# Converting half a weight matrix at a time, with two small edits to the planner and the last store

## The chip, the cores and the metric

The kernel runs on one core of a Trainium2 chip. The metric is the device time of one execution in microseconds; the median of three runs is shown. The engines named here are TensorE (PE in the profile, with its weight loads as PEld), VectorE (DVE), ScalarE (ACT), GpSimd (POOL) and SyncE (SP), which issues every data transfer of this kernel.

## The reference

A gated linear recurrence is followed by a multiplicative feed-forward block:

```python
# q, k, v, f_logit: (4, 8, 768, 48)
f = 1.0 / (1.0 + np.exp(-f_logit))
for t in range(S):
    state = f[:, :, t, :, None] * state + np.einsum('bhd,bhe->bhde', k[:, :, t], v[:, :, t])
    y[:, :, t] = np.einsum('bhd,bhde->bhe', q[:, :, t], state)
x = y.transpose(0, 2, 1, 3).reshape(3072, 384)
a = x @ w1              # w1, w2: (384, 1024)
b = x @ w2
h = a * b @ w3          # w3: (1024, 1024)
out = h @ w_out         # w_out: (1024, 384)
```

The weights arrive as 64-bit floats (w1, w2, w3 and w_out are products of a random float32 array with a numpy float64 scalar), q, k, v and f_logit as 32-bit floats.

## The kernel before

**Stages.** The sequence is cut into 24 units of 128 steps (`NU`), six for each of four batches. For a unit, `front` (line 474) issues the loads of f, k, q and v, makes the gate on ScalarE (L515), runs two scans on VectorE (L523 forward, L545 backward) and scales k and q with them (L553, L539); the pair products follow on TensorE (L566, L576), a causal mask on GpSimd (L706), the values (L650, L669), the state update (L683; L756, L759, L815 on VectorE) and a move of the result into `xt`, the transposed input of the feed-forward block. Units 0 to 3 come first and close together; units 0 and 1 have forms of their own (L604, L610, L622, L871).

Four units make a block of 512 tokens; there are six blocks. Block 0 does its up products plainly (`part`, line 916): for each of eight groups of columns and each half of the tokens one product with w1, whose result ScalarE copies (L931), and one with w2, multiplied into the copy on VectorE (L936). Blocks 1 and 2 use seven products in place of eight (`seven`, line 969, products at L990); blocks 3 to 5 use a longer scheme with shared sums (`many`, line 1117, products at L1145, kept results at L1166, sums at L1189). `three` (line 890) is the helper whose matmul is at L894, used by block 0's up products and by all `down` products (line 1225). w3 and w_out are folded into one matrix `wc` on TensorE first (L1477), so that the down step is one product by `wc`; VectorE makes four sums of it (L1523) and ten of w1 and w2 (L1509).

**Weights.** `fetch` (line 1367) loads a piece of 64-bit words into a large tile called `place` and turns it into 32-bit floats by four instructions: ScalarE makes the low bits (L1415, `rest`); VectorE shifts the high words into a region of magnitudes (L1418, `shifted`), joins sign and low bits into the destination (L1422, `signed`), and adds the magnitudes to it (L1428, `joined`). `weights` (line 1447) calls it for w1 and w2, which are read as four halves: A is columns 0 to 511 of w1, B the same of w2, C and D the other columns of w1 and w2. Each half is three pieces of 128 rows and 512 columns (`KM` = 3). `EARLY = "23ACBD"` gives the order in which VectorE takes units 2 and 3 and the four halves. Pieces take their places in `place` from the list `halves`, ten places of 1024 words; a load waits for the `signed` step of whoever had an overlapping place (`holders`, line 1363). `folding` (line 1462) does the same for four pieces of w_out (768 columns) and eight of w3 (1024 columns), at `2048 * ((load_no + 1) % NRAW)`.

**The order.** All work is given to `Plan` as tasks with a cost, dependencies and a priority; `listed` (line 181) repeatedly takes the task that could start first, ties going to the lower priority number, and so fixes each engine's order. The chip's real waits are semaphores between the instructions in that order. Transfers go to SP's queue and take one of eight lanes, weight loads also one of three heavy lanes (`moves`, line 461). `plan.pool("t", ...)` hands out the places for the kept results of `many`; `temporary` (line 384) maps its first four numbers to `firsts` and `ups`, which the sevens use too. Where the plan leaves TensorE idle in the first 130 us, `idle` (L396) emits products of a constant, one for each 0.43 us of the planned gap, each of two instructions.

The end: `down(i)` writes two output tiles of 128 rows, `o1` and `o2`; `store` (line 1308) sends each by one transfer. In the last one m3, the last product, is emitted together with a read of the flag `left` into a register of every engine.

Of the kernel before, what the change touches and what calls it, by code (L numbers as in the profile page):

```python
# [36 lines left out]
F32 = mybir.dt.float32  # L37
# [45 lines left out]
EARLY = "23ACBD"  # L83
CROWDED = [(6.0, 19.5, (1.35, 1.85)), (33.0, 46.0, (1.3, 1.3))]
# [190 lines left out]


def up_weights(w12, which, kc, jc):

    return w12[:, which, kc, jc * P : jc * P + P]
# [12 lines left out]
def ranged(ctx, tc, q, k, f_logit, v, w1, w2, w3, w_out, out, ident, w12, wc, left):  # L292
# [47 lines left out]
    halves = [a + i for a in (0, 2048, 4096, 8192, 10240) for i in (0, 1024)]  # L340
# [30 lines left out]
    plan.slot("ab", 4)  # L371
    moving = plan.add("PE", 0.0, lambda: None, takes=["ab"], prio=-1e9)
# [101 lines left out]
    def front(u):  # L474
# [4 lines left out]
        ask = [ask, ask + 0.5, ask + 1.0, n0 - (28.2, 28.2, 28.2, 28.2, 12)[min(u, 4)] if u in (0, 1) or u > 3 else ask + 1.2]  # L479
# [419 lines left out]
    def ffn(n):  # L899
# [190 lines left out]
        def w_view(i):  # L1090

            if i < KM * 4:
                return w12[:, :, i // 4].rearrange("p w (h g b c) -> p w h g b c", h=2, g=2, b=2)[:, :, i % 4 // 2, :, i % 2]
            return home(W_SUMS[i - 4 * KM][3]).rearrange("p (w g c) -> p w g c", w=2, g=2)
# [130 lines left out]
        def down(i):  # L1225
# [82 lines left out]
            def store(half):  # L1308
                def emit():
                    t0 = n * TB + (i + half * UB // 2) * P  # L1310
                    nc.sync.dma_start(out[t0 : t0 + P], q["o1" if half == 0 else "o2"])
                return emit
# [32 lines left out]
            for half, deps in ((1, ("c21", "c22")), (0, ("c11", "c12"))):  # L1345
                stores.append(moves(1, 197, 300, store(half), [q[nm] for nm in deps], -10))
# [20 lines left out]
    def fetch(loads_, a, prio, subs, deps=()):  # L1367

        total = subs[-1][1]
        if not wide:
            def plain():
                for place_, src in loads_:
                    for c0, c1, dst, _, _ in subs:
                        d = dst().rearrange("p (a m) -> p a m", a=a)
                        m = (c1 - c0) // a
                        b0 = c0 // a if len(subs) > 1 else 0  # L1380
                        nc.sync.dma_start(d[place_], src[:, :, b0 : b0 + m])
            waits = [d for sub in subs for d in sub[4]]
            ld = plan.add("SP", 1.9 * total / 512, plain, waits, prio, lag=2.0)
            return [ld] * len(subs)
        load_no = len(users)
        if load_no < 2 * 2 * KM:
            where = halves[load_no % len(halves)]
        else:
            where = 2048 * ((load_no + 1) % NRAW)
        raw = at(where, 2 * total).bitcast(U32)  # L1390
        words = raw.rearrange("p (n two) -> p n two", two=2)
        held = holders(where, 2 * total)

        def load():
            for place_, src in loads_:
                nc.sync.dma_start(raw.rearrange("p (a m) -> p a m", a=a)[place_], src.bitcast(U32))

        ld = moves(1, total, 400, load, held + list(deps), prio, SURE, lanes=("lane", "heavy"))
        asked.append(ld)
        got = []  # L1400
        users.append((where, 2 * total, got))
        ends = []

        def sub(c0, c1, dst, due, waits):
            n = c1 - c0
            w = n / 512
            lo, hi = words[:, c0:c1, 0], words[:, c0:c1, 1]
            a0 = spot[0] if n <= 512 else (spot[0] + 512) // 1024 * 1024 % 2048
            spot[0] = (a0 + (512 if n <= 512 else 1024)) % 2048
            m = magnitudes[:, a0 : a0 + n]  # L1410
            mine = range(a0 // 512, (a0 + n + 511) // 512)
            s = {}

            def rest():
                nc.scalar.activation(lo.bitcast(F32), lo, AF.Copy, bias=2.0, scale=2.0**-51)  # L1415

            def shifted():
                nc.vector.tensor_scalar(m.bitcast(U32), hi, 3, None, ALU.logical_shift_left)  # L1418

            def signed():  # L1420
                s["to"] = dst()
                nc.vector.scalar_tensor_tensor(  # L1422
                    s["to"].bitcast(U32), hi, 0x80000000, lo, ALU.bitwise_and, ALU.bitwise_or
                )

            def joined():
                to = s["to"].bitcast(I32)
                nc.vector.tensor_tensor(to, m.bitcast(I32), to, ALU.add)  # L1428

            past = [joins[i] for i in mine if i in joins]  # L1430
            e = plan.add("ACT", 0.2 + 0.43 * w, rest, [ld], due)
            h = plan.add("DVE", 0.16 + 0.27 * w, shifted, [ld] + past, due, shared=True)
            g = plan.add("DVE", 0.16 + 0.53 * w, signed, [e, h] + list(waits), due)
            j = plan.add("DVE", 0.16 + 0.53 * w, joined, [h, g], due - 1, shared=True)
            parts.append((g, j))
            joins.update({i: j for i in mine})
            got.append(g)
            ends.append(j)

        for one_ in subs:  # L1440
            sub(*one_)
        return ends

    def w12_part(which, kc, c0):
        return lambda: w12[:, which, kc, c0 : c0 + KH * P]

    def weights():
        due = dict(zip(((0, 0), (1, 0), (0, 1), (1, 1)), DUE))
        pieces.update({key: [] for key in due})
        for item in (x for x in EARLY if x in "ABCD"):  # L1450
            half, which = divmod("ABCD".index(item), 2)
            w = (w1, w2)[which]
            if True:
                for kc in range(KM):
                    c0 = half * KH * P
                    src = w[kc * P : kc * P + P, c0 : c0 + KH * P].unsqueeze(1)
                    pieces[which, half] += fetch(
                        [(slice(0, P), src)], 1, turn_of("ABCD"[2 * half + which]) + 0.02 * kc,
                        [(0, KH * P, w12_part(which, kc, c0), due[which, half] + 0.02 * kc, [])],
                    )  # L1460

    def folding():
        done = []
        for i in range(0, KF, 2):
            src = w_out[i * P : (i + 2) * P].rearrange("(kc p) c -> p kc c", p=P)
            done += fetch([(slice(0, P), src)], 2, 25 + 2.2 * i, [(
                0, 2 * DM, lambda i=i: wos[:, i : i + 2].rearrange("p a c -> p (a c)"), 45 + 2.2 * i,
                holders(10240, KF * DM) + [tk[3][nm] for nm in "qvs"],
            )], [tk[3]["z"]] if BEHIND and i < BEHIND else [])
# [23 lines left out]
        for jc in range(KF):  # L1493
            src = w3[jc].unsqueeze(1)
            got = fetch([(slice(0, P), src)], 1, 36 + 6 * jc, [(
                0, KF * P, w3_piece(jc), 50 + 6 * jc, fp[jc - 2 : jc - 1] if jc >= 2 else holders(8192, 2048),
            )])
# [4 lines left out]
        def sum_up(i, which):  # L1502
            def emit():
                t = w12t[:, which]
                b11, b21, b31, b12, b22, b32 = (
                    w12[:, which, kc, half * KH * P : half * KH * P + KH * P] for half in range(2) for kc in range(KM)
# [143 lines left out]
def convert(ctx, tc, w1, w2, w3, w_out, w12, wc):  # L1650
# [21 lines left out]
    for which, w in enumerate((w1, w2)):  # L1672
        for kc in range(KM):
            single(w[kc * P : kc * P + P], w12[:, which, kc])
# [347 lines left out]
```

## Time and profile before

| | us |
|---|---|
| median of 3 runs | 464.27 (464.22 to 465.06) |
| the profiled execution, its own time | 464.53 |
| its span, first to last instruction | 462.80 |
| PE busy | 454.1 |
| DVE busy | 364.8 |
| ACT busy | 208.2 |
| POOL busy | 64.7 |
| first product of the feed-forward block (L894) | 31.36 |
| end of the last product | 458.1 |

The profile is of one execution. A line of a timeline or of the chain gives the start and the duration in us, the engine, the tile, the line of the kernel and how many instructions are merged; in a group of instructions the last number is the mean in ns of one. "issue" is time in which the engine waited for nothing that the profile shows. Fillers (L396) count as busy.

### The profile page before, as it was taken

What the parts mean: (1) busy time and instruction counts of PE and PEld (TensorE: products, weight loads), DVE (VectorE), ACT (ScalarE), POOL (GpSimd) and SP (SyncE); (2) the same over time, 40 slices, a digit from 0 to 9 for tenths busy, and PEclk for the clock granted to TensorE, in tenths of its full rate; (3) what the DMA queues carried; (4) which work ended last, traced back from release to release, by engine and by line L of the source; (5) the groups of instructions that cost most, each with busy time, mean ns of one, the idle gap of its engine ahead of it and who ended that gap; (6) DMA issues with size and microseconds to landing.
All of it is one profiled execution on the core that took longest, in us unless ns stands there. A gap on an engine that the chain in (4) does not pass through costs nothing.

```text
span 462.8 us, 11767 instructions
## 1 busy us (share of the span) xinstructions
PE 454.1 (98%) x4800; PEld 395.6 (85%) x4800; DVE 364.8 (79%) x657; ACT 208.2 (45%) x468; POOL 64.7 (14%) x90
## 2 busy tenths in 40 slices
PE   8999999999999999999999999999999999999995
PEld 6778885666899888889998889998889988889995
DVE  8998999999898999989983598894669377767641
ACT  4565344532234444442432356664654666675000
POOL 9330001121122332322322000000000000000000
PEclk9999999999999999999999999999999999999999
DMA  6899899743246764445424335634135623330111
GB/s 181 269 297 306 268 343 276 260 103 87 80 110 192 205 186 113 133 135 166 120 57 113 111 112 178 221 113 149 47 124 176 200 91 92 90 95 0 35 68 40
DMA packets 43165, 68.75 MB, mean 149 GB/s; under 512 B 5201, under 2 KB 28242, under 8 KB 42082
## 3 DMA queue, kind: packets, MB, share of 16 engines
q1 hardware_dynamic: 43106, 67.95, 48.0%
q8 instruction: 39, 0.64, 0.6%
q14 instruction: 20, 0.16, 0.1%
HBM read 58.88 MB, written 9.04 MB: 147 GB/s over the span
## 4 chain that ended last, share of the span: by engine, by line
PE 93%; POOL 2%; DVE 2%; issue 1%; ACT 0%; POOLq 0%; DVEq 0%
PE f L894 26%; PE f L990 14%; PE f L1145 10%; PE f L1477 9%; PE pa L1145 7%; PE py L1145 5%; PE py L894 3%; PE py L650 3%; PE pa L894 3%; PE pa L576 2%; PE pa L683 2%; PE f L590 2%; PE py L669 2%; PE pa L990 1%; POOL ab L434 1%; PE f L396 1%
## 5 line engine op out<-in xcount | busy, mean ns | idle before, releaser
L706 POOL TENSOR_SCALAR_AFFINE_SELECT A<-A 64x512 f32<-64x512 f32 (+1 forms) x46 | 43.4, 943 | 104.0 <-ACT A L700 101.9
L1477 PE MATMUL f<-place 128*128 128x384 f32 x128 | 42.7, 488 | 0.0
L894 PE MATMUL f<-xt,w 128*128 128x256 f32 x192 | 42.1, 380 | 0.0
L894 PEld LDWEIGHTS f<-xt,w 128*128 128x128 f32 x192 | 36.3, 190 | 5.0
L894 PE MATMUL f<-place 128*128 128x192 f32 x216 | 39.5, 328 | 0.0
L1477 PEld LDWEIGHTS f<-place 128*128 128x128 f32 x128 | 23.8, 190 | 15.3
L894 PEld LDWEIGHTS f<-place 128*128 128x128 f32 x216 | 35.4, 190 | 0.5 <-issue 0.2
L990 PE MATMUL f<-xt,w 128*128 128x256 f32 x132 | 34.2, 379 | 0.0
L545 DVE TENSOR_TENSOR_SCAN bwd<-gate,back 112x512 f32<-112x512 f32 x24 | 30.8, 1285 | 0.7
L523 DVE TENSOR_TENSOR_SCAN fwd<-gate,floor 112x512 f32<-112x512 f32 x24 | 30.5, 1271 | 1.1 <-ACT gate L515 0.3
L990 PEld LDWEIGHTS f<-xt,w 128*128 128x128 f32 x132 | 24.8, 190 | 3.1
L842 ACT ACTIVATE ys<-py 112x512 f32<-112x512 f32 x22 | 13.1, 596 | 28.2 <-PE py L669 28.2
L1415 ACT ACTIVATE place<-place 128x512 f32<-128x512 uint32 (+2 forms) x24 | 21.1, 890 | 10.1 <-DMA place<-in_w_dram 7.9
L894 PE MATMUL f<-wc,ab 128*128 128x192 f32 x128 | 23.4, 326 | 0.0
L990 PE MATMUL f<-place 128*128 128x256 f32 x84 | 22.4, 385 | 0.0
L806 POOL TENSOR_TENSOR G<-lasts,gate 112x4 f32<-112x4 f32 x20 | 10.7, 535 | 81.3 <-ACT lasts L528 50.3
L894 PEld LDWEIGHTS f<-wc,ab 128*128 128x128 f32 x128 | 21.4, 190 | 0.4
L515 ACT ACTIVATE gate<-f 112x512 f32<-112x512 f32 x22 | 13.9, 632 | 15.4 <-DVE bwd L545 6.6
L650 PEld LDWEIGHTS py<-A,vt 64*64 64x64 f32 (+1 forms) x672 | 13.3, 127 | 7.3 <-issue 5.6
L650 PE MATMUL py<-A,vt 64*64 64x64 f32 (+1 forms) x672 | 18.1, 223 | 0.2
L1552 ACT ACTIVATE A<-A,back 128x512 f32<-128x512 f32 x23 | 17.9, 778 | 0.3
L990 PEld LDWEIGHTS f<-place 128*128 128x128 f32 x84 | 15.3, 190 | 2.2 <-ACT place L1031 0.2
(345 smaller groups left out, 1046.4 us busy)
## 6 DMA issues: line engine op xcount, KB each, us to landing
place<-in_w_dram SPq DMA_DIRECT2D x21, 512.0 KB, 6.4
A<-in_w_dram SPq DMA_DIRECT2D x19, 512.0 KB, 4.0
place<-in_w_dram SPq DMA_DIRECT2D x8, 1024.0 KB, 6.9
out_dram<-o SPq DMA_DIRECT2D x24, 192.0 KB, 2.3
q<-in_q_dram SPq DMA_DIRECT2D x46, 96.0 KB, 3.0
vt<-in_v_dram SPq DMA_DIRECT2D x23, 192.0 KB, 3.2
k<-in_k_dram SPq DMA_DIRECT2D x44, 96.0 KB, 2.5
yt<-ys SPq DMA_DIRECT2D x44, 96.0 KB, 2.9
```

The costliest lines, as they stand in the source:

```text
L515: nc.scalar.activation(gate[u % 2][:, 0:NQ], fu, AF.Sigmoid)
L523: nc.vector.tensor_tensor_scan(s["P"], gate[u % 2][:, 0:NQ], floor, 0.0, ALU.mult, ALU.max)
L545: nc.vector.tensor_tensor_scan(s["R"][:, ::-1], gate[u % 2][:, NQ:0:-1], back[:, ::-1], 0.0, ALU.mult, ALU.max)
L650: done = nc.tensor.matmul(y_block(u, hp, par, half)[p0 : p0 + w], lhsT=s["v"][half * W : half * W + W, h * D : h * D + w], rhs=s["A"][half ...
L706: nc.gpsimd.affine_select(out=a, in_=a, pattern=pattern, compare_op=ALU.is_ge, fill=0.0, base=0, channel_multiplier=-1,)
L842: nc.scalar.activation(ys, py, AF.Copy, accum_out=ysum[:, u : u + 1])
L894: nc.tensor.matmul(out_, lhsT=lhs[i], rhs=rhs[i], start=start and i == 0, stop=i == len(lhs) - 1, skip_group_check=True,)
L990: nc.tensor.matmul(q[nm][:, which * TH : which * TH + TH], lhsT=lhs[i](which), rhs=rhs[i], start=start and which == 0 and i == 0, stop=i = ...
L1145: nc.tensor.matmul(banks[g, c][:, which * TH : which * TH + TH], lhsT=lhs, rhs=x_node(a), start=first and which == 0, stop=True, skip_grou ...
L1415: nc.scalar.activation(lo.bitcast(F32), lo, AF.Copy, bias=2.0, scale=2.0**-51)
L1477: nc.tensor.matmul(w3s["p", jc], lhsT=w3s[jc][:, kc * P : kc * P + P], rhs=wos[:, kc], start=(kc == 0), stop=(kc == KF - 1),)
L1552: return lambda: nc.scalar.activation(a, a, AF.Sign, bias=small, accum_out=counts[:, i : i + 1])
```

## The change

- `fetch` takes a list of loads and converts them together. Each load still has its own transfer and its own ScalarE step; `shifted`, `signed` and `joined` are one instruction each over all the columns. For w1 and w2 this is 1536 columns in place of three times 512; for w_out and w3 there is one load, as before.
- `w12` is laid out by matrix, half, row block and column, so that a half is contiguous; `up_weights`, `w_view`, `sum_up` and `convert` follow.
- The halves have fixed places, `EARLY_AT`: A and D at 0, C at 3072, B at 8192. `halves` goes. The places of w_out and w3 are the same numbers as before, written out.
- v of unit 3 is asked for behind A's loads and not ahead of them (`VLATE`).
- The first four places of the pool `t` are taken by `aside` until the last two sevens of block 2 have ended.
- The output tile that is stored last goes in two transfers: columns 0 to 191 when `c11` is done, and the others when `c12` is.

```diff
+VLATE = (1.2, 2.05)
+EARLY_AT = {"A": 0, "C": 3072, "B": 8192, "D": 0}
...
-    w12 = const.tile([P, 2, KM, DFF], F32, name="w12")
+    w12 = const.tile([P, 2, 2, KM, KH * P], F32, name="w12")
...
-    halves = [a + i for a in (0, 2048, 4096, 8192, 10240) for i in (0, 1024)]
...
+    aside = plan.add("none", 0.0, lambda: None)
+    plan.pools["t"][0:4] = [aside] * 4
...
-        ask = [ask, ask + 0.5, ask + 1.0, n0 - (28.2, 28.2, 28.2, 28.2, 12)[min(u, 4)] if u in (0, 1) or u > 3 else ask + 1.2]
+        ask = [ask, ask + 0.5, ask + 1.0, n0 - (28.2, 28.2, 28.2, 28.2, 12)[min(u, 4)] if u in (0, 1) or u > 3 else ask + VLATE[u - 2] if u in (2, 3) else ask + 1.2]
...
+            if n == MANY - 1:
+                for q in s["seven"][-2:]:
+                    for nm in ("e11", "e22", "e21", "e12"):
+                        q[nm]["frees"].append(aside)
...
+                if final and half == 0:
+                    stores.append(moves(1, 98, 300, store(0, 0, DH), [q["c11"]], -10))
+                    stores.append(moves(1, 98, 300, store(0, DH, DM), [q["c12"]], -10))
+                    continue
                 stores.append(moves(1, 197, 300, store(half), [q[nm] for nm in deps], -10))
...
-    def fetch(loads_, a, prio, subs, deps=()):
+    def fetch(loads_, where, prio, due, dst, waits=(), deps=()):
...
+        landed, low = [], []
+        for i, (at_, n, src) in enumerate(loads_):
+            def load(at_=at_, n=n, src=src):
+                nc.sync.dma_start(raw[:, 2 * at_ : 2 * (at_ + n)].rearrange("p (a m) -> p a m", a=src.shape[1]), src.bitcast(U32))
+
+            def rest(at_=at_, n=n):
+                part_ = lo[:, at_ : at_ + n]
+                nc.scalar.activation(part_.bitcast(F32), part_, AF.Copy, bias=2.0, scale=2.0**-51)
+
+            landed.append(moves(1, n, 400, load, held + list(deps), prio + 0.02 * i, SURE, lanes=("lane", "heavy")))
+            asked.append(landed[-1])
+            low.append(plan.add("ACT", 0.2 + 0.43 * n / 512, rest, [landed[-1]], due + 0.02 * i))
...
+        h = plan.add("DVE", 0.16 + 0.27 * w, shifted, landed + past, due, shared=True)
+        g = plan.add("DVE", 0.16 + 0.53 * w, signed, [*low, h] + list(waits), due)
+        j = plan.add("DVE", 0.16 + 0.53 * w, joined, [h, g], due - 1, shared=True)
...
+            pieces[which, half] = fetch(
+                [(kc * KH * P, KH * P, w[kc * P : kc * P + P, cols].unsqueeze(1)) for kc in range(KM)],
+                EARLY_AT[item], turn_of(item), due[which, half],
+                lambda which=which, half=half: w12[:, which, half].rearrange("p k c -> p (k c)"),
+            )
```

More of the change, by code (lines that the diff above doesn't have):

```diff
@@ L277, in up_weights @@
 def up_weights(w12, which, kc, jc):
-    return w12[:, which, kc, jc * P : jc * P + P]
+    return w12[:, which, jc // KH, kc, jc % KH * P : jc % KH * P + P]
 def place_of(jc):
@@ L1092, in w_view @@
             if i < KM * 4:
-                return w12[:, :, i // 4].rearrange("p w (h g b c) -> p w h g b c", h=2, g=2, b=2)[:, :, i % 4 // 2, :, i % 2]
+                return w12[:, :, i % 4 // 2, i // 4].rearrange("p w (g b c) -> p w g b c", g=2, b=2)[:, :, :, i % 2]
             return home(W_SUMS[i - 4 * KM][3]).rearrange("p (w g c) -> p w g c", w=2, g=2)
@@ L1306, in c12, with store @@
                 nc.vector.tensor_tensor(q["o1"][:, DH:DM], q["Z"], dns["u2"], ALU.add)
-            def store(half):
+            def store(half, c0=0, c1=DM):
                 def emit():
                     t0 = n * TB + (i + half * UB // 2) * P
-                    nc.sync.dma_start(out[t0 : t0 + P], q["o1" if half == 0 else "o2"])
+                    nc.sync.dma_start(out[t0 : t0 + P, c0:c1], q["o1" if half == 0 else "o2"][:, c0:c1])
                 return emit
@@ L1365, in holders @@
         return [g for a, m, gs in users if a < where + n and where < a + m for g in gs]
-    def fetch(loads_, a, prio, subs, deps=()):
-        total = subs[-1][1]
+    def fetch(loads_, where, prio, due, dst, waits=(), deps=()):
+        total = sum(n for _, n, _ in loads_)
         if not wide:
             def plain():
[L1376 to L1389, printed above, removed]
+                d = dst()
+                for at_, n, src in loads_:
+                    nc.sync.dma_start(d[:, at_ : at_ + n].rearrange("p (a m) -> p a m", a=src.shape[1]), src)
+            return [plan.add("SP", 1.9 * total / 512, plain, list(waits), prio, lag=2.0)]
@@ L1390, in fetch @@
         raw = at(where, 2 * total).bitcast(U32)
-        words = raw.rearrange("p (n two) -> p n two", two=2)
+        pairs_ = raw.rearrange("p (n two) -> p n two", two=2)
+        lo, hi = pairs_[:, :, 0], pairs_[:, :, 1]
         held = holders(where, 2 * total)
[L1394 to L1398, printed above, removed]
@@ L1399, in fetch @@
-        asked.append(ld)
         got = []
         users.append((where, 2 * total, got))
[L1402 to L1445, printed above, removed]
+        landed, low = [], []
[8 more added lines that the diff above has]
+            low.append(plan.add("ACT", 0.2 + 0.43 * n / 512, rest, [landed[-1]], due + 0.02 * i))
@@ new lines, in fetch, with shifted, signed @@
+        w = total / 512
+        a0 = spot[0] if total <= 512 else (spot[0] + 512) // 1024 * 1024 % 2048
+        if a0 + total > 2048:
+            a0 = 0
+        spot[0] = (a0 + (total + 511) // 512 * 512) % 2048
+        m = magnitudes[:, a0 : a0 + total]
+        mine = range(a0 // 512, (a0 + total + 511) // 512)
+        s = {}
+        def shifted():
+            nc.vector.tensor_scalar(m.bitcast(U32), hi, 3, None, ALU.logical_shift_left)
+        def signed():
+            s["to"] = dst()
+            nc.vector.scalar_tensor_tensor(
+                s["to"].bitcast(U32), hi, 0x80000000, lo, ALU.bitwise_and, ALU.bitwise_or
+            )
@@ new lines, in joined @@
+        def joined():
+            to = s["to"].bitcast(I32)
+            nc.vector.tensor_tensor(to, m.bitcast(I32), to, ALU.add)
+        past = [joins[i] for i in mine if i in joins]
+        h = plan.add("DVE", 0.16 + 0.27 * w, shifted, landed + past, due, shared=True)
+        g = plan.add("DVE", 0.16 + 0.53 * w, signed, [*low, h] + list(waits), due)
+        j = plan.add("DVE", 0.16 + 0.53 * w, joined, [h, g], due - 1, shared=True)
+        parts.append((g, j))
+        joins.update({i: j for i in mine})
@@ L1447, in weights @@
+        got.append(g)
+        return [j]
     def weights():
         due = dict(zip(((0, 0), (1, 0), (0, 1), (1, 1)), DUE))
-        pieces.update({key: [] for key in due})
         for item in (x for x in EARLY if x in "ABCD"):
@@ L1452, in weights @@
             w = (w1, w2)[which]
[L1453 to L1460, printed above, removed]
+            cols = slice(half * KH * P, (half + 1) * KH * P)
+            pieces[which, half] = fetch(
+                [(kc * KH * P, KH * P, w[kc * P : kc * P + P, cols].unsqueeze(1)) for kc in range(KM)],
+                EARLY_AT[item], turn_of(item), due[which, half],
+                lambda which=which, half=half: w12[:, which, half].rearrange("p k c -> p (k c)"),
+            )
     def folding():
@@ L1465, in folding @@
             src = w_out[i * P : (i + 2) * P].rearrange("(kc p) c -> p kc c", p=P)
[L1466 to L1469, printed above, removed]
+            done += fetch(
+                [(0, 2 * DM, src)], 2048 * ((13 + i // 2) % NRAW), 25 + 2.2 * i, 45 + 2.2 * i,
+                lambda i=i: wos[:, i : i + 2].rearrange("p a c -> p (a c)"),
+                holders(10240, KF * DM) + [tk[3][nm] for nm in "qvs"], [tk[3]["z"]] if BEHIND and i < BEHIND else [],
+            )
         w3s = {}
@@ L1494, in folding @@
             src = w3[jc].unsqueeze(1)
-            got = fetch([(slice(0, P), src)], 1, 36 + 6 * jc, [(
-                0, KF * P, w3_piece(jc), 50 + 6 * jc, fp[jc - 2 : jc - 1] if jc >= 2 else holders(8192, 2048),
-            )])
+            got = fetch(
+                [(0, KF * P, src)], 2048 * ((17 + jc) % NRAW), 36 + 6 * jc, 50 + 6 * jc, w3_piece(jc),
+                fp[jc - 2 : jc - 1] if jc >= 2 else holders(8192, 2048),
+            )
             fp.append(plan.add("PE", 5.15, fold(jc), got + done + fp[-1:], 0, takes=["f"]))
@@ L1505, in emit @@
                 b11, b21, b31, b12, b22, b32 = (
-                    w12[:, which, kc, half * KH * P : half * KH * P + KH * P] for half in range(2) for kc in range(KM)
+                    w12[:, which, half, kc] for half in range(2) for kc in range(KM)
                 )
@@ L1673, in convert @@
         for kc in range(KM):
-            single(w[kc * P : kc * P + P], w12[:, which, kc])
+            for half in range(2):
+                single(w[kc * P : kc * P + P, half * KH * P : (half + 1) * KH * P], w12[:, which, half, kc])
     rows_ = keep.tile([P, KF, DM], F32, name="rows")
```

## The prediction

> **What bounds the kernel.** I read the page's busy shares and slices first. TensorE is busy for 98% of the span, the granted clock never drops, and no slice between the second and the last falls under 9.
>
> ```profile
> PE 454.1 (98%) x4800; PEld 395.6 (85%) x4800; DVE 364.8 (79%) x657; ACT 208.2 (45%) x468; POOL 64.7 (14%) x90
> ...
> PE   8999999999999999999999999999999999999995
> ...
> DVE  8998999999898999989983598894669377767641
> ...
> PEclk9999999999999999999999999999999999999999
> ```
>
> VectorE is nearly as busy in the first third, but a busy TensorE sets the end. So the second view is the chain of waits in order of time: where is TensorE *not* doing products that the result needs? L396 is the filler, products of a constant[...]; a filler occupies TensorE's queue whether or not its reason still holds.
>
> ```profile
> 23.81 1.35 PE f L871 x12
> 25.17 1.30 PE f L396 x6
> 26.46 0.44 PE py L650 x12
> ...
> 28.41 0.86 issue
> 29.27 0.60 PE pa L683 x20
> 29.87 1.49 PE f L396 x6
> 31.36 2.59 PE f L894 x12
> ```
>
> From 31.36 on, the feed-forward products (L894 and the folds L1477) run gapless; there are three more losses, 0.86 us of filler at 124.78, about 0.5 us at 336.95, and the tail after the last product at 458.1:
>
> ```profile
> 118.11 6.67 PE f L894 x30
> 124.78 0.86 PE f L396 x4
> ...
> 336.95 0.46 issue
> 337.41 0.60 ACT ys L1166
> ...
> 456.78 1.31 PE pa L894 x8
> 458.10 0.02 issue
> 458.12 0.36 DVE o L1306
> ```
>
> So an edit gains only if it moves 31.36 forward, or shortens one of these three. The work itself (as many products as before) does not change.
>
> **Merged conversions.** The third view is VectorE's timeline. A, the first half of w1, is three pieces; the last step of the third ends at 29.26 + 0.69 = 29.95.
>
> ```profile
> 22.95 0.68 DVE L539 TENSOR_TENSOR Q<-place,fwd 112x512 f32<-112x512 f32 x1
> 23.56 0.42 DVE L1418 TENSOR_SCALAR place<-place 128x512 uint32<-128x512 uint32 x1
> ...
> 29.26 0.69 DVE L1428 CUSTOM_DVE_ANT_0 w<-place,w 128x1024 uint16<-128x1024 uint16 x1
> ```
>
> Cost of a step by size, from the groups by shape (512, 768, 1024 columns): shift 419, 552, 681 ns; sign 683, 950, 1220; join 719, 953, 1225. Each 256 columns add about 131, 268 and 270. At 1536 columns that makes 0.94 + 1.76 + 1.76 = 4.46 us, against 3 x (0.419 + 0.683 + 0.719) = 5.46 for three pieces. Neighbouring steps overlap (piece starts at 34.92 and 36.58, 1.66 apart, for a sum of 1.82), so the real saving is nearer 5.0 - 4.25 = 0.75 us per half, 3 us of VectorE over the four. ScalarE's three steps per half stay as they are.
>
> The merge adds waits: the shift now needs all three pieces landed, the sign all three ScalarE steps. Behind them on VectorE stand the state updates of unit 2 (L756, L759, L815). VectorE is busy with unit 3's Q until 23.6 in any case, and A's third ScalarE step starts by 24.98 and ends by 25.6. I lay it out: shift 23.56 to 24.43, unit 2's three updates (0.35 + 0.36 + 0.68) to 25.75, sign to 27.45, join to 29.15. A is ready **0.8 us earlier** than 29.95. If the third piece came after 24.4 this would shrink one for one.
>
> For C and B the margin is larger: TensorE has four products of 1.3 us from A, four from C and a visit (1.4) before it needs B, so at 31.36 + 10.4 + 1.4 = 43.1; B ended at 40.97 + 0.69 = 41.66. Their 1.5 us saved is worth nothing on the path.
>
> **What A's 0.8 us buys.** Before, A was ready at 29.95, yet TensorE began at 31.36: it came to the end of unit 3's products at 29.87 and then had 1.49 us of filler. The number of fillers is the planner's gap divided by 0.43. Working its rules through by hand (for order and filler counts alone; the times are the trace's): A's loads go out one transfer earlier, so its second ScalarE step is placed ahead of the copy of unit 2's scores, which puts unit 2's visit (L650) some 0.5 later in the plan: four fillers at 25.17 in place of three; and A's readiness then stands 0.9 us behind unit 3's end in place of 1.48: two fillers in place of three. A filler is two instructions of 0.216. On the chip: 25.17 + 1.74 (filler), 1.38 (visit), 2.03 (unit 3 with its 0.86 stall), about 1.0 (filler) = 31.3; without the stall 30.45.
>
> The stall of 0.86 is "issue": it stands in the middle of a run of small products and waits for nothing that the profile shows. Instruction blocks come by DMA (q8, 39 packets, 0.64 MB, 16 KB each) through rings then full of weight loads. The Trainium skill ("Runtime: NRT & Kernel Launch", Instruction fetch mechanics) says that crossing a block's boundary is mostly hidden, which speaks against fetching as the cause. By that rule there is no fetch to overlap, the stall stays at its 0.86 and the start at 31.3; by the row, if it is a late block, a filler more ahead of it (0.43) hides as much of it and the start comes at 30.9. I take the row's reading: **-0.45 us**, ends 0 and -0.9.
>
> **Loads.** v of unit 3 goes from ahead of A's three loads to behind them: one issue (0.43 on SP) and 192 KB moved past three. It landed about 4.3 us after its issue at 13.81; behind 1.5 MB (landing by about 22.5) it comes some 5 us later, and is read at 28.1 (L683). Five us of cover; one us beyond would cost one. D's loads now all wait for A's sign step (27.5), before their turn at 32.7: nothing. But places of 3072 columns make w_out's first load, at 2048, wait for D's sign step rather than C's. It went out at 41.88; D's third ScalarE step ended at 44.82 + 0.66 = 45.5, and one sign step of 1.76 behind it makes 47.3, 5.4 us later. w_out's fourth load takes the same place after it; the third waited for D before too (issued 49.57) and comes sooner. Behind the waiting load on SP's queue stand unit 4's f, k and q, wanted only after 68. Cover for w_out: folding starts at 67.9 with five products of block 0 in reserve (those at 118.11). They fill TensorE while VectorE makes the sums of the folded weight, which end at 121.15, so a delay of up to 124.78 - 121.15 = 3.6 us at the fold is free. I cost it at 0, ends 0 and +2.
>
> **The filler at 124.78.** The first down product waits for VectorE's last product of block 0 (L936 at 124.90, 0.42). It must follow the last up product whatever is saved. With VectorE up to 3 us ahead the step may stand less queued; one filler of two drops out at best: **-0.2**, ends -0.86 and +0.4.
>
> **Temporaries.** Before, the planner thought four places free while the sevens used them; the first ScalarE copies into them (278.66 and 284.70) waited for TensorE alone, so the mistake cost nothing there. Giving places out in another order can undo or renew the stall at 336.95, a copy that waited for its place: **-0.2**, ends -0.5 and +0.3.
>
> **Last store.** After the final add ends at 458.48 the store is issued (332 ns), and takes 2.7 to landing; the span ends at 462.80. Halved, it has 96 KB for 192; the other half leaves at about 453.3, while SP waits for `left` anyway.[...] Rows of 96 KB (2.5 to 3.3 medians) against out's 2.3 at 192 KB show no gain at all, though those landed among heavy traffic. I take **-0.25**, ends 0 and -0.4.
>
> **Sum.** -0.45 - 0.2 - 0.2 - 0.25 = -1.1 us. The profiled execution took 464.53 (span 462.80 and 1.73 around it), so 463.4; from the median 464.27, 463.15, and I say **463.1**.
>
> **Rivals.** (1) *Start not moved*, 25%: fillers and stall hold TensorE as before (31.3 above); only the store gains: 464.0. For it: both fillers are fixed counts and A was already waiting at 29.95. Against: A's 0.8 us makes the second count smaller. (2) *Everything falls out*, 17%: stall gone (-0.86), filler at 124.78 gone (-0.86), place stall gone (-0.46), store -0.3: -2.5, 461.8. For it: none is tied to work. Against: a list planner fills one gap and opens another. (3) *The fold comes late*, 7%: w_out's first load goes out 5.4 us later, its conversions of some 2.3 us follow, and the first fold waits; beyond the 3.6 us of cover it costs one for one. At 6 us late, +2.4 and -0.5 elsewhere: 466.2. Against: VectorE is 3 us ahead by then.
>
> **From chances to numbers.** Forecast 51% (its own range 462.6 to 463.6). What a measurement of this kernel can tell from no change is 0.2%, 0.93 us: faster is under 463.34. The forecast's share below that is about four fifths (0.42), with rival 2 0.17 and a little of rival 1: 0.64. Same: the rest of both, 0.29. Slower 0.07. The range reaches to rival 2's 461.8 and past rival 1, 464.4.
>
> **What would show it.** VectorE's 1536-column steps of 0.94, 1.76, 1.76; A's join ending at 29.15; L396 x8 near 25.2 and x4 near 30; the first L894 at 30.9; the issue stall shorter than 0.86; the last store landing 2.4 after issue. Wrong would be an L894 start at 31.3 or later, or TensorE idle between 65 and 125.

## The result: 0.4% faster, and where the profile shows it

The changed kernel took 463.24 us (median of 17 runs, 462.6 to 464.57) against 465.05 for the kernel before in the same comparison; the ratio is 0.996, 95% interval 0.9942 to 0.9978. In a second comparison (the first experiment below) it was 463.48 against 464.50, ratio 0.9973 (0.9962 to 0.9985). The forecast of 463.1 stands, its range too. The profiled execution of the changed kernel was one of its longer ones, 464.25 with a span of 462.52, so it shows only 0.3 us of the difference; the repeat (span 461.25) shows 1.55.

The page of the changed kernel, busy shares and slices:

```profile
span 462.5 us, 11749 instructions
...
PE 452.9 (98%) x4800; PEld 395.5 (86%) x4800; DVE 362.1 (78%) x633; ACT 208.6 (45%) x468; POOL 63.9 (14%) x90
...
PE   7999999999999999999999999999999999999995
```

VectorE has 24 instructions and 2.7 us fewer. TensorE sets the end as before. The line numbers have moved: L399 is the filler, L897 the product that was L894, L686 unit 3's state products, L1415, L1419 and L1425 the shift, sign and join.

The chain of waits of the changed kernel, start and duration in us, at the start of the feed-forward products, at the last filler, and at the end:

```profile
25.17 1.73 PE f L399 x8
26.90 0.44 PE py L653 x13
...
28.84 0.04 issue
28.88 0.67 PE pa L686 x26
29.55 1.06 PE f L399 x4
30.61 3.89 PE f L897 x18
...
118.60 5.38 PE f L897 x24
123.98 0.86 PE f L399 x4
...
452.06 5.21 PE f L897 x32
457.28 0.02 issue
457.30 0.36 DVE o L1313
```

The fillers are eight and four instructions, as worked out. The stall of 0.86 is 0.04. The first feed-forward product comes 0.75 us earlier than before, the last one ends 0.82 us earlier (457.28 against 458.10), so nearly nothing was gained between. The filler at 124 is still there. What follows the last product took 5.2 us in this execution against 4.7 before.

VectorE's timeline of the changed kernel, for half A:

```profile
23.89 0.96 DVE L1415 TENSOR_SCALAR place<-place 128x1536 uint32<-128x1536 uint32 x1 [0.25 <-DMA place<-in_w_dram]
24.77 0.35 DVE L759 TENSOR_TENSOR A<-pa,S 112x192 f32<-112x192 f32 x1
...
26.21 1.75 DVE L1419 SCALAR_TENSOR_TENSOR w<-place 128x1536 uint32<-128x1536 uint32 x1
27.99 1.76 DVE L1425 CUSTOM_DVE_ANT_0 w<-place,w 128x3072 uint16<-128x3072 uint16 x1
```

The steps take 0.96, 1.75 and 1.76, against 0.94, 1.76 and 1.76 extrapolated. The shift waited 0.25 for the third piece. A is ready at 29.75, 0.2 earlier than before and not 0.8: the shift started 0.33 later than laid out, the sign step at 26.21 in place of 25.75, and sign and join did not overlap as assumed. A was ready 0.86 us before the first feed-forward product took it (30.61), so on the chip its readiness did not set the start; the fillers did.

In what follows, *first* is the start of the first feed-forward product, *stretch* the time from there to the end of the last product, and *tail* the rest of the span. They are read from the records of each profile; first is up to 0.2 below the chain's number, because the chain starts an instruction where the one before it ends.

| | first | stretch | tail |
|---|---|---|---|
| before | 31.20 | 426.88 | 4.72 |
| changed | 30.44 | 426.82 | 5.26 |
| changed, again | 30.43 | 426.41 | 4.40 |

### The profile page after: what moved, and what is told of

The parts are those of the page before. It is cut to its first block, busy times and chain, and to the rows that moved or that the text cites. A ratio compares the mean times of both kernels' runs of the same rounds, so it can differ in the third digit from the quotient of the medians.

```text
span 462.5 us, 11749 instructions
## 1 busy us (share of the span) xinstructions
PE 452.9 (98%) x4800; PEld 395.5 (86%) x4800; DVE 362.1 (78%) x633; ACT 208.6 (45%) x468; POOL 63.9 (14%) x90
## 4 chain that ended last, share of the span: by engine, by line
PE 94%; POOL 2%; DVE 2%; issue 0%; POOLq 0%; DVEq 0%
PE f L897 25%; PE f L993 15%; PE f L1148 11%; PE f L1464 9%; PE py L1148 6%; PE pa L1148 5%; PE py L897 4%; PE pa L897 4%; PE py L653 3%; PE pa L579 2%; PE pa L686 2%; PE f L593 2%; PE py L672 2%; PE py L993 1%; POOL ab L437 1%; PE f L399 1%
## 5 line engine op out<-in xcount | busy, mean ns | idle before, releaser
L709 POOL TENSOR_SCALAR_AFFINE_SELECT A<-A 64x512 f32<-64x512 f32 (+1 forms) x46 | 42.3, 920 | 110.6 <-ACT A L703 108.5
L897 PE MATMUL f<-xt,w 128*128 128x256 f32 x192 | 42.1, 380 | 0.0
L897 PEld LDWEIGHTS f<-xt,w 128*128 128x128 f32 x192 | 36.3, 190 | 5.0
L1464 PEld LDWEIGHTS f<-place 128*128 128x128 f32 x128 | 23.9, 190 | 15.5
L993 PE MATMUL f<-xt,w 128*128 128x256 f32 x140 | 36.2, 380 | 0.0
L897 PE MATMUL f<-place 128*128 128x192 f32 x192 | 34.8, 327 | 0.0
L897 PEld LDWEIGHTS f<-place 128*128 128x128 f32 x192 | 31.5, 190 | 0.3 <-issue 0.2
L993 PEld LDWEIGHTS f<-xt,w 128*128 128x128 f32 x140 | 26.3, 190 | 3.5
L897 PE MATMUL f<-wc,ab 128*128 128x192 f32 x128 | 23.6, 328 | 0.0
L897 PEld LDWEIGHTS f<-wc,ab 128*128 128x128 f32 x128 | 21.3, 190 | 0.4
L1262 DVE TENSOR_TENSOR place<-ab 128x512 f32<-128x512 f32 x24 | 16.5, 689 | 1.0 <-PE f L897 0.9
```

Source lines behind the costliest of these rows:

```text
L709: nc.gpsimd.affine_select(out=a, in_=a, pattern=pattern, compare_op=ALU.is_ge, fill=0.0, base=0, channel_multiplier=-1,)
L897: nc.tensor.matmul(out_, lhsT=lhs[i], rhs=rhs[i], start=start and i == 0, stop=i == len(lhs) - 1, skip_group_check=True,)
L993: nc.tensor.matmul(q[nm][:, which * TH : which * TH + TH], lhsT=lhs[i](which), rhs=rhs[i], start=start and which == 0 and i == 0, stop=i = ...
L1262: nc.vector.tensor_tensor(abs_[j], x, y, op)
L1464: nc.tensor.matmul(w3s["p", jc], lhsT=w3s[jc][:, kc * P : kc * P + P], rhs=wos[:, kc], start=(kc == 0), stop=(kc == KF - 1),)
```

## The experiments

My theory going in: the time is the first product's start, plus a stretch that is nearly fixed work, plus the tail; the stall ahead of the first product is a late block of TensorE's instructions. The main rival: the 3 us of VectorE that merging saves are the gain, wherever in the span they fall.

**The changed kernel again.** No edit; it gives the other runs something to stand beside.

> The changed kernel once more, on the chip of the runs beside it. Theory (the gain is an earlier first feed-forward product, 0.75 us in the profiles, and a shorter last store): ratio 0.996 to 0.998, first product of L897 at 30.6 again and no stall over 0.3 us ahead of it. Rival (the gain lies in VectorE's relief spread over the span): the first product anywhere, and the stretch from it to the last product shorter than the 426.7 us of both profiles.

Ratio 0.9973 (0.9962 to 0.9985), 463.48 us. First at 30.43, no stall (0.07), as expected. The stretch was 426.41, 0.4 below both earlier profiles: in the first profile of the changed kernel TensorE paused 0.3 us in a run of small products at 208 us, and here it did not.

**The last tile in one store.**

```diff
-                if final and half == 0:
-                    stores.append(moves(1, 98, 300, store(0, 0, DH), [q["c11"]], -10))
-                    stores.append(moves(1, 98, 300, store(0, DH, DM), [q["c12"]], -10))
-                    continue
```

> The changed kernel with its last output tile stored in one transfer again. Theory: the last store takes 2.7 us from issue to landing in place of about 2.4, so 0.25 us slower than the changed kernel (+0.05%). Rival (the fixed part of a transfer is all of it): no difference. Rival (the store is most of the gain that the medians show and the profiles do not): 1 us slower.

463.54 us against 463.48 with two: no difference that the runs can tell. The profile's tail was 4.52 against 4.40. Over all 14 profiles of this study the tails with one store are 4.52, 4.57, 4.72 and 4.77 (median 4.65), with two 4.23 to 4.50 in eight and 5.04 and 5.26 in two (median 4.42). That would be 0.2 us for the split, with a scatter of more than four times as much. In the long tails a few of the store's packets come late: those of the changed kernel began at 458.51 and the last ended at 460.51, against 458.10 and 459.12 in the repeat. Packets of the two instruction queues ran at the same time, but they did so in the repeat too, so what made them late isn't shown. The rival, which puts the whole 1 us on the split, is out.

What the run shows besides is a stall of 0.63 in a program whose first 450 us are the same as in the run before it:

```profile
28.80 0.10 PE pa L686 x3
28.90 0.63 issue
29.53 0.67 PE pa L686 x26
30.19 1.06 PE f L399 x4
31.25 3.89 PE f L897 x18
```

**Three instructions for each merged step, planned anew.** Everything else as changed: layout, places, load order, temporaries, stores.

```diff
-        h = plan.add("DVE", 0.16 + 0.27 * w, shifted, landed + past, due, shared=True)
-        g = plan.add("DVE", 0.16 + 0.53 * w, signed, [*low, h] + list(waits), due)
-        j = plan.add("DVE", 0.16 + 0.53 * w, joined, [h, g], due - 1, shared=True)
...
+        def convert_(i, at_, n):
...
+        for i, (at_, n, src) in enumerate(loads_):
+            convert_(i, at_, n)
```

`convert_` makes the shift, sign and join of one piece three tasks of their own.

> The changed kernel with each piece of 512 columns converted by its own three VectorE instructions; layout, places, loads, temporaries and stores as changed. Theory: A is ready about 0.2 to 0.8 us later than in the changed kernel's profile (29.75), the planner's fillers follow, the first L897 product comes at 30.6 to 31.4, so 0 to 0.8 us slower. Rival (merging is worth its 3 us of VectorE): 1.5 us or more slower.

466.71 us (the profiled execution, 467.8, was its longest), ratio to before 1.0047 (1.0032 to 1.0061): 3.2 us slower than the changed kernel, slower than the kernel before, and a miss for my theory. The rival's number fits. But the profile doesn't show VectorE as the place: first 31.16 (with a stall of 0.63), and a stretch of 429.87, longer by 3.5. In the chain, the folds end at 122.48 in place of about 117, with fewer up products left behind them, then six filler instructions in place of four, and four waits for a place or a bank (a slot of TensorE's output memory) in the last 200 us where the changed kernel has one wait of 0.74:

```profile
122.48 1.29 PE f L897 x6
...
127.25 1.31 PE f L399 x6
...
279.38 0.59 ACT Q L1169
...
380.01 0.46 issue
380.46 0.60 ACT Q L1169
...
404.91 0.46 issue
405.36 0.60 ACT ys L1169
...
413.32 0.46 issue
413.78 0.87 ACT A L1545 x2
...
416.45 0.60 ACT Q L1169
```

At each of the four TensorE pauses 0.46 to 0.84 us for ScalarE's copy, 2.2 in all. So of the 3.5 some 1.5 is in these pauses and 0.4 in the fillers; the rest is spread over delays of 0.1 to 0.2 between products. These places are far from the conversion of w1 and w2. The planner had other tasks and costs and made another order of everything. To know what merging itself is worth, the order has to be held.

**Three instructions for each merged step, in the changed kernel's order.** The tasks and costs stay those of the merged steps; only what they emit is split.

```diff
         def shifted():
-            nc.vector.tensor_scalar(m.bitcast(U32), hi, 3, None, ALU.logical_shift_left)
+            for a, n, _ in loads_:
+                nc.vector.tensor_scalar(m[:, a : a + n].bitcast(U32), hi[:, a : a + n], 3, None, ALU.logical_shift_left)
...
```

`signed` and `joined` are split in the same way.

> The changed kernel in its own order of tasks, with each merged VectorE step emitted as three instructions of 512 columns in a row; everything else as changed. Theory (pieces lost 3.2 us because the planner, given other costs and tasks, made another order, with its waits for places and its fewer reserve products at the end of the folds): A is ready some 0.5 to 0.8 us later, the fillers hide part of that, so 0 to 0.8 us slower than the changed kernel, and the stretch from first to last product stays at 426.4 to 426.9 us. Rival (the three extra VectorE microseconds are what costs): 466 to 467 us again and a stretch near 429.9.

465.86 us (462.87 to 470.16, the widest scatter here; the profiled execution took 464.75), ratio to before 1.0031 (1.0015 to 1.0046). Slower than the changed kernel by 2.4, three times what I had allowed. The stretch was 427.88, neither theory's 426.9 nor the rival's 429.9. The excess in this profile, 1.1 to 1.5 over the changed kernel's two, stands in one place. The waits between 30 and 40 us, and GpSimd's timeline there:

```profile
PEld py L653 <- POOL A L709: 1.3, 1, 1.3
PE py L653 <- POOL A L709: 1.2, 1, 1.2
...
30.56 5.55 POOL L709 TENSOR_SCALAR_AFFINE_SELECT A<-A 64x512 f32<-64x512 f32 x2 [4.73 <-ACT A L703]
```

Unit 3's mask, which GpSimd makes in place, took 5.55 us; it took 1.98 in the profile of the changed kernel and 3.52 in its repeat, where TensorE had work until then. VectorE's three sign, three join and two shift instructions ran back to back from 31.23 to 35.58; the second half of the mask lasted from 31.27 to 36.11. So there was a third theory: what three instructions cost is the mask's turn. The run planned anew does not have this loss, though it has as many VectorE instructions:

```profile
31.02 2.83 POOL L709 TENSOR_SCALAR_AFFINE_SELECT A<-A 64x512 f32<-64x512 f32 x2 [4.75 <-ACT A L703]
```

There VectorE takes the sign and the join of one piece in turn, as in the kernel before (mask 2.17). In both the mask came to an end after a sign step, and the join that needs that sign took 1.02 in place of 0.69. With three signs ahead of three joins no join has to wait for its own sign.

**The same, with C's sign step told to follow the mask.**

```diff
+    pieces[0, 1][0]["deps"][1]["deps"].append(tk[3]["c"])
     ready_at = 0.0
     for t in plan.order():
```

> The run with three instructions per VectorE step in the changed kernel's order, and one dependency more: C's sign step waits for unit 3's mask on GpSimd. Theory (the 2.4 us lost there come from that mask, which took 5.55 us beside back-to-back VectorE steps where it takes 2.0 beside the merged ones, and from TensorE's wait of 1.3 us for it): the mask takes 1.4 to 2.8 us, TensorE does not wait for it at 34.8, the spread of the runs shrinks to about 1.5 us, and the time is 463.3 to 464.3. Rival (three more microseconds of VectorE cost, wherever): 465.5 or more again.

467.64 us (465.68 to 470.13). This did not test it: the planner's dependency orders emission, and since sign step and mask share no data, no semaphore came of it. VectorE's sign step started at 31.30, beside the mask, which took 5.86; TensorE paused 1.7 us for it (starts apart), and then its granted clock fell. It stands as a second sample of the run before.

**The same, with a semaphore.** The first of C's sign instructions waits for the mask, by the helper that the kernel uses for TensorE's row tiles. The planner's dependency of the run before stays in.

```diff
                 done = nc.vector.scalar_tensor_tensor(
...
+                if due == 24.0 and a == 0:
+                    ordered(done, st[3]["masked"])
```

> Three instructions per VectorE step in the changed kernel's order, and now a real wait: the first of C's three sign instructions waits on a semaphore for unit 3's mask on GpSimd. In the run before it, the added dependency only told the planner, and VectorE did not wait. Theory (the 2.4 us lost with three instructions come from the mask, which cannot run beside back-to-back VectorE steps that read two operands): the mask takes 1.4 to 2.2 us in place of 5.6 to 5.9, TensorE has no wait over 0.4 us near 34.5, and the time is 463.3 to 464.5. Rival (three more microseconds of VectorE cost, wherever): 465.5 or more.

463.48 us, ratio to before 0.9983 (0.9972 to 0.9994): 2.4 us faster than the same order without the wait, 4.2 faster than the run before it, from which it differs by the semaphore alone, and level with the merged kernel. The mask took 1.37 us:

```profile
31.71 1.37 POOL L709 TENSOR_SCALAR_AFFINE_SELECT A<-A 64x512 f32<-64x512 f32 x2 [5.81 <-ACT A L703]
...
33.12 1.90 DVE L1421 SCALAR_TENSOR_TENSOR w<-place 128x512 uint32<-128x512 uint32 x3 [0.69 <-POOL A L709]
```

VectorE stood 0.69 us for the mask, has all 24 instructions that merging takes away, and nothing is lost that the runs can tell. So in this order VectorE's microseconds show no worth on the path; the merged steps are worth up to 2.4 us because they leave GpSimd a turn. (This profile had a stall of 1.42 at 28.86; it is the longest of the kernel's runs but one.)

**The sevens' places given out from the start, as before.** The six lines of `aside` are taken out.

> The changed kernel with the four places of the sevens given out from the start, as before. Theory (the places cost nothing where they were taken early, but the order of the last 200 us is solved anew): the stretch from first to last product differs by 0 to 1 us either way, the stall of a copy that waits for its place moves, and the first product stays at 30.6. Rival (the wrong places cost waits at the start of block 3): 0.5 to 1.5 us slower with VectorE or ScalarE waiting between 275 and 300 us.

463.28 us, ratio to before 0.9971 (0.9960 to 0.9982), stretch 426.97. No wait of the kind the rival wanted, and no difference in time. What `aside` is for shows in the last run below.

**The kernel before, one filler more.**

```diff
-                idle(n)
+                idle(n + 1 if 25.5 < t["at"] < 26.5 else n)
```

> The kernel before with four fillers in place of three ahead of unit 2's visit; nothing else. Theory (the 0.86 us stall inside unit 3's state products is a late block of TensorE's instructions, so a filler ahead of it runs in time that was lost anyway): the visit starts at 26.9 in place of 26.46, the stall shrinks to 0.2 to 0.5, and the first feed-forward product still comes at 31.2 to 31.4. Rival (the stall has another cause and stays): first product at 31.8, 0.43 us slower.

464.74 us, ratio 1.0005 (0.9992 to 1.0018). The stall was 0.07 and the first product came at 30.93, 0.27 earlier than before with one filler more. The rival's 31.8 is out. Part of this is luck: TensorE went on at 28.94, against 29.27 before, and a filler can cover a wait but not end it sooner.

**The changed kernel without fillers.** Once without those after 29 us, once without any after 20 us.

```diff
-            if ready_at and n:
+            if ready_at and n and t["at"] < 29.0:
```

> The changed kernel without the fillers ahead of the first feed-forward product and ahead of the first down product (two matmuls each). Theory: the products start when their data is ready, 29.85 in place of 30.61 and 124.6 in place of 124.84: 1.0 us faster than the changed kernel. Rival (the fillers do what they are for): the granted clock falls after the gap, or the stall of instruction blocks returns, and nothing is gained.

> The changed kernel with no filler at all after 20 us: eight filler matmuls fewer ahead of unit 2's visit than the kernel without late fillers, which keeps them. Theory (late block of instructions): the visit starts at 26.1, the stall inside unit 3's state products grows to about 0.8 to 1.0, those products end near 29.5, and A's readiness sets the first product at 30.0 to 30.2, so no time is gained on the kernel without late fillers. Rival: no stall, unit 3's products end at 28.7, and A still sets 30.0 to 30.2; the time is the same, the stall tells them apart.

Without the late fillers: 462.87 us, ratio to before 0.9966 (0.9953 to 0.9979), against 463.48: 0.6 faster, where 1.0 was expected. It is the fastest of all, though the intervals overlap. First at 30.12, right after A's last step (28.21 + 1.76 = 29.97); at 124 nothing came of it, since the second down product then waited for VectorE's sums until 125.80:

```profile
119.87 3.90 PE f L897 x18
...
125.05 0.70 DVE place L1262
125.75 0.04 issue
125.80 1.24 PE f L897 x6
```

The clock stayed.

Without any after 20 us: 463.30, ratio 0.9971 (0.9947 to 0.9995). Unit 2's visit started at 26.05, and the stall was back, 0.73 us. TensorE's timeline, first of the kernel before, then of this run:

```profile
28.13 0.27 PE L683 MATMUL pa<-place,kt 64*48 64x48 f32 x5
29.27 0.60 PE L683 MATMUL pa<-place,kt 64*64 64x48 f32 x27 [0.86 <-issue]
...
27.78 0.39 PE L686 MATMUL pa<-place,kt 64*48 64x48 f32 x11
28.90 0.55 PE L686 MATMUL pa<-place,kt 64*48 64x48 f32 x21 [0.73 <-issue]
29.81 1.53 PE L897 MATMUL f<-xt,w 128*128 128x256 f32 x6 [0.37 <-DVE w L1425]
```

TensorE came to these products 0.8 us sooner than in the changed kernel and went on at the same time, 28.9.

Where the pause stands says more. Before, it comes after five of unit 3's state products, with six filler instructions ahead of the visit; in the changed kernel's order after three, with eight; here after eleven, with none. Each makes eleven. In the records, all seven profiles with a stall of more than 0.3 us have it between the 347th and the 348th matmul, also the last run below, where another order has put other products (L670) there. So the pause belongs to a place in TensorE's stream of instructions, not to a product's data.

The records of transfers have one 16 KB packet on the instruction queue q8 near here; in every profile with a stall here, TensorE goes on 1.3 to 1.5 us after that packet's end:

| | packet ended | pause (starts apart) | went on | after |
|---|---|---|---|---|
| before | 27.92 | 1.08 | 29.27 | 1.35 |
| one store | 28.05 | 0.85 | 29.53 | 1.48 |
| pieces | 28.06 | 0.85 | 29.60 | 1.54 |
| same order | 27.74 | 0.56 | 29.13 | 1.39 |
| no filler after 20 | 27.60 | 0.95 | 28.90 | 1.30 |
| mask with a semaphore | 28.93 | 1.64 | 30.29 | 1.36 |
| merge only | 29.11 | 2.28 | 30.56 | 1.46 |

The other seven have 0.3 us or nothing between these two matmuls, and pass there 1.3 to 1.8 us after the packet, all but one: in the repeat of the changed kernel TensorE went on 1.07 after it (27.80). So the delay isn't a constant. By the fixed place and the seven rows the stall is a late block of instructions. No run moved the packet by itself, so that the block waited for this packet, and what made the packet late, are not shown. Among the rows the resumption varies by 1.7 us, from one execution to the next.

From the 348th matmul to the first feed-forward product it is 1.93 us before and 1.56 in all eight profiles that have four filler instructions there in place of six, with a stall or without. This 0.37 is what the change gains at the start where a late block holds up both kernels; the rest of the 0.75 is that TensorE went on at 28.88 in place of 29.27.

**v of unit 3 ahead of A's loads, as before.** `VLATE = (1.2, 1.2)`.

> The changed kernel with v of unit 3 loaded ahead of A's pieces, as before. The planner then sets three and three fillers at the start, as before, and none at 124. Theory (fillers and a late block of instructions set the start; the rest is the planner's order): the stall is 0.5 to 0.9 us again, the first product comes at 31.0 to 31.4 though A is ready at about 29.8, and the filler at 124 is saved (0.3 to 0.9): within 0.5 us of the changed kernel. Rival (the load order is what makes the changed kernel faster): 1 us or more slower than it.

464.00 us, ratio to before 0.9993 (0.9983 to 1.0002): by the medians 0.5 slower than the changed kernel, by the ratios 0.9, past what my theory gave. Its parts were half wrong. The planner set three and three fillers and none at 124, as expected; there was no stall, and the first product came at 30.13. But the stretch was 427.56, 1.1 longer: TensorE paused at 41.9 for ScalarE's copy out of a bank, and at 264, 412 and 442 for steps of other engines. An early start was paid back.

**Merging, layout and places alone.** `VLATE = (1.2, 1.2)`, no `aside`, one last store.

> Merged conversions, layout and places of the change alone: v of unit 3 first, the last tile in one store, the sevens' places given out from the start. Theory (the gain over the kernel before is its new order and the start, not one of the small edits): ratio to before 0.996 to 0.999, like the changed kernel. Rival (the small edits bring the gain): ratio 0.999 to 1.002.

464.78 us, ratio 1.001 (0.9988 to 1.0032): nothing gained. In this order the planner puts a kept result of the last blocks into `firsts` 18 us before the last seven ends, and that seven writes over it, so the output is wrong; the instructions are the same. That is what `aside` prevents. By the interval the rival fits and my theory doesn't, but the profile is of a disturbed start, which shows what the stall can do. TensorE's timeline:

```profile
28.20 0.29 PE L670 MATMUL py<-Q,S 48*48 48x64 f32 x5
30.56 0.56 PE L670 MATMUL py<-Q,S 48*48 48x64 f32 x10 [2.07 <-issue]
...
31.58 2.93 PE L397 MATMUL f<-floor 112*128 112x256 f32 x6
34.30 1.91 PE L895 MATMUL f<-xt,w 128*128 128x256 f32 x4
```

Six filler instructions took 2.93 here, 1.56 in the same view of the kernel before. The busy times of the stretches from 28 to 45 us, with the columns stretch, its length, then PE, PEld, DVE, ACT and POOL with their counts, the granted clock, the DMA share and GB/s:

```profile
28.00:31.00 3.00, 0.93 (x37) 0.78 (x41) 2.26 (x3) 0.30 (x1) 2.56 (x2) 0.89 0.75 248
31.00:37.00 6.00, 6.00 (x36) 4.78 (x29) 4.75 (x4) 1.81 (x4) 0.26 (x1) 0.50 0.64 178
37.00:45.00 8.00, 7.90 (x95) 6.64 (x94) 3.63 (x4) 4.84 (x11) 0.00 (x0) 0.99 0.78 222
```

After a stall of 2 us the clock was 0.50 for 6 us: 3 us of work lost, more than the stall. The profiled execution took 468.63, the second longest of its 14; the median doesn't have this loss.

## Why the prediction was right, and where it was wrong

**What bounds it**: right. In every run TensorE's work is the stretch, and the times differ by the start and by pauses in it.

**Merged conversions**: the step costs were within 0.02 us. A's 0.8 us earlier was 0.2, for the third piece's transfer and the later sign step. Its value on the path was put at nothing for C, B and D, and the run with a semaphore shows no worth for all four: 24 more instructions and the same time. What the prediction did not see is GpSimd. It named no GpSimd step that VectorE could hold up, and beside unsplit steps nothing shows; beside split ones in the same order the mask costs 2.4 us.

**The start**: fillers four and two, right to the instruction, though A came only 0.2 earlier: the counts come from the planner's costs, not from the chip. Of the two readings of the stall I took the trace's, a late block, at -0.45 with ends of 0 and -0.9. The runs speak for the block, by its fixed place: the Trainium skill ("Runtime: NRT & Kernel Launch", Instruction fetch mechanics) has a block's boundary mostly hidden, and here it cost 0 to 2.1 us, which is often not hidden. The -0.45 was the filler less behind the block, and that is 0.37 in the profiles. What comes on top is a lottery: in the profiles the start moved by -0.75; with a stall of 0.63 in the changed program (the run with one store) it moved by -0.1. A fourth filler alone, in the kernel before, gains nothing in time (1.0005), since what it hides it also takes.

**Loads, D's wait, w_out**: costed at 0; the folds in the changed kernel end 0.5 us later than before by the clock, though the products began 0.75 earlier (up products at 118.60 against 118.11, and six instructions fewer of them, 1.3 us of the reserve), inside the cover of 3.6. Rival 3 did not come about; in the run planned anew with pieces the reserve was used up and gave 0.4 us of filler more.

**Filler at 124**: put at -0.2, was 0. The step that failed: not VectorE's queue but the sums after it. Without the filler the next down product waited to 125.80.

**Temporaries**: -0.2. The stall at 336.95 went and one of 0.74 came at 354.39, TensorE waiting for three VectorE sums in a row. Zero in time with or without `aside`.

**Last store**: -0.25; the median tails differ by 0.2 between the two kinds of profiles, and the timed runs by nothing that they can tell. The size stays open.

**Sum**: -1.1 from 464.27 (which makes 463.17; the prediction has 463.15). Measured were 463.24 and 463.48: the second is -1.0 against the better-founded median of before beside it, 464.50, the first -1.8 in its own comparison. The number was right in part by luck: two of the four terms were zero, the store's is open, and the first was larger in the profiles by when a block came. The profiles account for 0.37 at the start and about 0.2 at the tail; what gives the rest of the 1.0 isn't settled: with the load order undone the gain is 0.0007, with only merging it is nil, and each of these is another order of the whole program. I can say that no single edit has been shown to carry it, and that the order that came out has short pauses.

## What to carry to other kernels

Where a planner lays out a whole program, an edit is compared with its order held fixed: three more instructions per step cost 3.2 us planned anew, 2.4 in the same order, and nothing that the runs can tell once one neighbour on another engine got its turn. A pause that waits for nothing in the profile, inside a run of small matmuls, is worth a count: if as many matmuls stand ahead of it in another order, it belongs to the stream of instructions, and the records of the instruction queue come next, before anything is moved to fill it. And a filler is work for the queue that holds it: it is as long as the planner's guess, not as the gap.

## What the runs showed of the hardware

- A block of TensorE's instructions can come late. The pause stood between the 347th and the 348th matmul in all seven profiles with a stall, 0.56 to 2.28 us between their starts, and TensorE went on 1.3 to 1.5 us after the end of a 16 KB packet of q8 that took 0.9 to 1.1 us; in one profile without a stall it was 1.07 after. In the kernel before the DMA engines were busy to 0.91 from 25 to 30 us; that this made the block late isn't shown.
- The granted clock halved after a stall of 2.07 us and stayed at 0.50 for 6 us (filler matmuls 427 ns apart in place of 216); after the stalls of 0.6 to 1.4 us at the same place it stayed at 1.00 from 31 to 45 us. When the pause fell at 35 us, for the mask (1.7 us), it was 0.87 from 34 to 38 and 0.70 from 38 to 42.
- GpSimd's mask beside back-to-back VectorE instructions, sign and join with two operands each, took 5.55 and 5.86 us, 1.37 after a wait. By the Trainium skill ("SBUF — State Buffer", Who interferes with whom) a VectorE instruction with two inputs in SBUF (the memory that the engines share) contends with a GpSimd instruction that reads it, over a shared pair of ports that is locked for one of the two at a time. Here the loser stood for some eight instructions in a row, and in the repeat of the changed kernel it slipped in after the sign step, whose join then took 2.09 in place of 1.76.
